# Nine chunks of keys for a tile's two heads, gates between transposes and masks, and exponentials ahead of a step's masks and signs, in a top-k attention kernel

## Chip, cores and metric

The kernel runs on one core of one Trainium2 chip. The metric is the device time of one execution in microseconds (us), as a median of several runs; lower is better. The engines are named as in the profile: PE (matmul) with its weight loads PEld, DVE (vector), ACT (activation), POOL (general), SP (issues the DMAs).

## The reference

Two blocks follow each other. Attention: for each of 8 batches and 8 heads, 576 queries and keys of 64 numbers; only the 32 largest scores of a row are kept. Then a mixture of 8 experts over the 4608 tokens of 512 numbers, where each expert keeps its 80 best tokens.

```python
scores = scale * np.matmul(q, k.transpose(0, 1, 3, 2))
kth = np.partition(scores, -top_k, axis=-1)[..., -top_k:-top_k + 1]
scores = np.where(scores >= kth, scores, -1000000000.0)
scores = scores - np.max(scores, axis=-1, keepdims=True)
attn = np.exp(scores)
attn = attn / (np.sum(attn, axis=-1, keepdims=True) + 1e-09)
x = np.matmul(attn, v)             # then (B, H, S, D) -> (B*S, H*D)
...
logits = x @ w_gate                # expert = argmax, gate = softmax there
h = np.maximum(x[tok_idx] @ w1[e], 0.0)
out[tok_idx] = gate_w[tok_idx, None] * (h @ w2[e])
```

## The kernel before, in words

The attention part works through 32 pairs of heads (n = 0 to 31: a batch and two of its heads). A pair has five tiles of queries, t = 0 to 4: four of 128 queries for both heads, and one, t = 4, that holds the last 64 queries of both heads on the two halves of the partitions. A unit is one tile of one head: nine units in a pair, 288 in all (`units` in `run`). The order is written out by hand, one `step(i)` per unit; stages of several units are interleaved, each with its lag, and no scheduler changes it. Because a pair has nine units, the stages fall on even steps in one pair and on odd steps in the next.

The stages of a tile:

- `turn` (L206): once a pair, q and k are turned by ten transposes (L204) into the score buffer `sp`, and ACT copies them out (`both`, L217). `load` and `load_v` fetch two pairs ahead on SP's queue.
- `front` (L219): eight matmuls in the trace (L229; four in the code) write the scores of both heads into `sp`, and ACT copies them into the tile `s` (L236). `sp` is made by `four` (L197): four of the eight PSUM banks, from a pool with one buffer. So fronts, turns of q and k, turns of xn and the gates' logits all take the same buffer in turn, each waiting until ACT has copied the last one out.
- `parts` and `search` (L239, L248): DVE finds the eight largest of six pieces of 96 scores (L244), from them the 24 largest of the row (L255, L263). ACT makes signs against the 24th with their sum (`sign`, L260), POOL multiplies scores and signs (`y`, L266), DVE takes the next eight (L268), and `pick` (L271) chooses the threshold.
- `below` (L275): marks the scores under the threshold, for units with odd numbers on ACT (L280) and for even ones on POOL (L282).
- `turn_w` (L302): turns the scores of the tile, keys onto partitions, by transposes (L318) into the PSUM tiles `ab` (four full chunks of 128 keys per head, one buffer) and `cc` (a fifth chunk per head, two buffers). For each head the fifth chunk takes the last 128 keys, so it overlaps the fourth by 64; the rows of V that stand for the overlap are zero. Then matmuls with the masks (L323) push the dropped scores down, and ACT takes the exponentials of `cc` (L325) and `ab` (L327) into `wT`.
- `back` (L330): forty matmuls in the trace (L338; twenty in the code) multiply `wT` with V. V has a column of ones, so the sum comes along; results lie in the same bank as `cc`.
- `over` and `divide` (L342, L352): DVE inverts the sum (`z`, L350); the product with it (`xn`) is on DVE for t = 0 and 1 (L359), on ACT for the others (L367). Only then is the buffer of `cc` free.
- `norm` (L369): when a pair is complete, writes xn to memory, turns it (L204, `sp` again; copied out at L384), multiplies by the gate's weights (L389, `sp`; copied out at L396) and hands over to `gates` on DVE.

A step first walks a string of letters: "GybGcGdGeGGzaxg" in odd steps, "GGbghHmMyGcGdGeGzax" in even ones. G is a piece of `parts`, a to h and H are parts of `search` of units at the lags in the table (e holds the sign, h and H the picks), y POOL's product, m a mask on ACT, M a mask on POOL, z `over`, x `divide`. So every step issues one sign on ACT, and every even step a mask on ACT before it. After the string come `turn_w` of the unit six steps back, `front` for four steps ahead, `back` of the unit seven steps back (ahead of `turn_w` for t = 4), a `turn` if no front was due, then a part of `norm`. `turn_w` and `front` stand in the same step; it is an odd one in even pairs (the string has a sign), an even one in odd pairs (mask and sign), with t = 4 the other way round. In the step after it `back` and a turn follow: q and k after t = 1, xn of the pair before after t = 2; the logits come after t = 4.

ACT's queue in order is therefore, for one tile: [mask] sign, xn, exponentials of cc and ab, s, and in the next step [mask] sign, and both or xT.

```python
back = dict(a=0, b=1, c=1, d=1, e=1, y=3, g=4, h=5, m=5, H=4, M=4)
for c in "GybGcGdGeGGzaxg" if i % 2 else "GGbghHmMyGcGdGeGzax":
    ...
if whole(i - LT):
    self.turn_w(*units[i - LT][:2])
```

After attention comes `finish`: routing on DVE, PE and POOL, then eight experts. The change does not touch it. A second, slow path (`lean`) is compiled as well and does not run with these inputs.

Of the kernel before, what the change touches and what calls it, by code (L numbers as in the profile page):

```python
# [21 lines left out]
FAR = 1e-30  # L22
HUGE = 2.0 ** 100
TINY = 2.0 ** -48
# [3 lines left out]
def kernel(  # L28
# [120 lines left out]
    class Attention:  # L149


        def __init__(self, stack, lean):
            self.lean = lean
            pool = lambda name, bufs, **kw: stack.enter_context(tc.tile_pool(name=name, bufs=bufs, **kw))
            self.nat, self.qkp, self.rows = pool("nat", 1), pool("qkp", 2), pool("rows", 2)
            self.small, vpool = pool("small", 7), pool("vpool", 1)
            self.ps_s, self.ps_w, self.ps_c = (pool(n, k, space=PSUM) for n, k in (("ps_s", 1), ("ps_w", 1), ("ps_c", 2)))
            self.qk, self.turned, self.lg = {}, {}, {}
            self.s, self.top, self.cnt, self.y, self.mask, self.w, self.xn = ({} for _ in range(7))
            self.thr, self.z = thr_all, z_all  # L160
            self.odd = set()


            self.vb = []
            for j in range(1 if lean else 3):
                t = vpool.tile([P, NK, 2, D + 1], F32, name=f"vb{j}")
                nc.gpsimd.memset(t[:, :, :, D : D + 1], 1.0)
                nc.gpsimd.memset(t[: P - TL, NF, :, :], 0.0)
                self.vb.append(t)

            self.xT = vpool.tile([P, NK * P], F32, name="xT")
            nc.gpsimd.memset(self.xT[:, S:], 0.0)
# [15 lines left out]
        def load_v(self, n, b, hp):  # L188
            one = bass.ds(b, 1)
            t = self.vb[n % len(self.vb)]  # L190
            for h in range(2):
                nc.sync.dma_start(
                    t[:, :NF, h, :D], v[one, 2 * hp + h, : NF * P, :].rearrange("o (c p) d -> p (o c) d", p=P))
            nc.sync.dma_start(
                t[P - TL :, NF, :, :D], v[one, 2 * hp : 2 * hp + 2, NF * P :, :].rearrange("o h p d -> p (o h) d"))

# [22 lines left out]
        def front(self, n, t):  # L219
# [10 lines left out]
            g = 2 if t < NF else 1  # L230
            s = self.rows.tile([P, 2 * S], F32, name="s", tag="s", bufs=2 if self.lean else 7)
            for h in range(g):
                self.s[i + h] = s[:, h * S : (h + 1) * S]
# [14 lines left out]
        def search(self, i):  # L248
# [24 lines left out]
            yield  # L273

        def below(self, i):  # L275

            self.top.pop(i)
            self.mask[i] = self.rows.tile([P, S], BF16, name="mask", tag="mask", bufs=4)
            if i in self.odd:
                nc.scalar.activation(self.mask[i], self.s[i], Act.Relu, bias=self.thr[:, i : i + 1], scale=-1.0)  # L280
                return
            nc.gpsimd.tensor_scalar(self.mask[i], self.s[i], self.thr[:, i : i + 1], None, op0=Alu.is_lt)  # L282

# [12 lines left out]
        def drop(self, i):  # L296

            s, top = self.s[i], self.top.pop(i)
            self.mask[i] = self.rows.tile([P, S], BF16, name="mask", tag="mask", bufs=2)
            nc.vector.tensor_scalar(self.mask[i], s, self.thr[:, i : i + 1], top[:, 0, 0:1], op0=Alu.is_lt, op1=Alu.add)  # L300

        def turn_w(self, n, t):  # L302

            i = n * UPP + 2 * t
            g = 2 if t < NF else 1
            if i == NU - 1 and not self.lean:

                ab = self.four().rearrange("p h (c r) -> p h c r", r=P)
            else:
                ab = self.ps_w.tile([P, 2, NF, P], F32, name="ab", tag="ab")  # L310
            cc = self.ps_c.tile([P, 512], F32, name="cc", tag="cc")
            keys = [slice(c * P, c * P + P) for c in range(NF)] + [slice(S - P, S)]
            dst = [[ab[:, h, c, :] for c in range(NF)] + [cc[:, h * P : (h + 1) * P]] for h in range(g)]

            for h in range(g):
                sc = self.s.pop(i + h)
                for c in range(NK):
                    nc.tensor.matmul(dst[h][c], lhsT=sc[:, keys[c]], rhs=ident, start=c == 0 or (c == NF and h == 0), stop=False,  # L318
                                     is_transpose=True, skip_group_check=True)
            for h in range(g):  # L320
                mk = self.mask.pop(i + h)
                for c in (NF, *range(NF)):
                    nc.tensor.matmul(dst[h][c], lhsT=mk[:, keys[c]], rhs=huge if i + h in self.odd else minus, start=False, stop=True, skip_group_check=True)  # L323
            wT = self.rows.tile([P, 2 * NK, P], F32, name="wT", tag="wT")
            nc.scalar.activation(wT[:, 2 * NF : 2 * NF + g, :].rearrange("p h r -> p (h r)"), cc[:, : g * P], Act.Exp,  # L325
                                 scale=scale / TINY)
            nc.scalar.activation(wT[:, : g * NF, :], ab.rearrange("p h c r -> p (h c) r")[:, : g * NF, :], Act.Exp, scale=scale / TINY)  # L327
            self.w[n, t] = wT, cc

        def back(self, n, t):  # L330

            wT, cc = self.w.pop((n, t))
            vb = self.vb[n % len(self.vb)]
            for h in range(2 if t < NF else 1):
                o = slice(2 * P + h * (D + 1), 2 * P + (h + 1) * (D + 1))
                for c in range(NK):
                    for r in range(0, P, TL):
                        nc.tensor.matmul(cc[r : r + TL, o], lhsT=wT[:, h * NF + c if c < NF else 2 * NF + h, r : r + TL],  # L338
                                         rhs=vb[:, c, h if t < NF else r // TL, :], start=(c == 0), stop=(c == NF))
            self.w[n, t] = cc  # L340

        def over(self, n, t):  # L342


            g = 2 if t < NF else 1
            sums = self.w[n, t][:, 2 * P : 2 * P + 2 * (D + 1)].rearrange("p (h d) -> p h d", h=2)[:, :g, D]
            z = self.z[:, n % NP, t, :g]
# [4 lines left out]
        def divide(self, n, t):  # L352
            if t == 0:
                self.xn[n] = self.rows.tile([P, NK, 2, D], F32, name="xn", tag="xn")
            cc = self.w.pop((n, t))
            if t < 2:

                sums = cc[:, 2 * P : 2 * P + 2 * (D + 1)].rearrange("p (h d) -> p h d", h=2)[:, :, :D]
                nc.vector.tensor_tensor(out=self.xn[n][:, t, :, :], in0=sums, op=Alu.mult,  # L359
                                        in1=self.z[:, n % NP, t, :].unsqueeze(2).to_broadcast([P, 2, D]))  # L360
                return
            for h in range(2):
                if t < NF:
                    p, o, j, m = slice(0, P), 2 * P + h * (D + 1), h, P
                else:
                    p, o, j, m = slice(TL * h, TL * h + TL), 2 * P, 0, TL
                nc.scalar.activation(self.xn[n][:m, t, h, :], cc[p, o : o + D], Act.Copy, scale=self.z[p, n % NP, t, j : j + 1])  # L367

        def norm(self, n, b, hp, bi, nb, cs=range(NK)):  # L369
# [14 lines left out]
            nc.scalar.copy(xT[:, at], ps[:, at])  # L384
            yield 1
            lp = self.four()[:, 0, : NK * E].rearrange("p (c e) -> p c e", e=E)
# [49 lines left out]
        def run(self, slow):  # L436
# [14 lines left out]
            def whole(i):  # L451

                return 0 <= i < NU and units[i][2] > 0

            def step(i, last):
# [11 lines left out]


                back = dict(a=0, b=1, c=1, d=1, e=1, y=3, g=4, h=5, m=5, H=4, M=4)
                for c in "GybGcGdGeGGzaxg" if i % 2 else "GGbghHmMyGcGdGeGzax":  # L470
                    if c == "G":
                        if 0 <= i < NU:
                            next(first[i])
                    elif c == "a":
                        if 0 <= i < NU:
                            next(first[i], None)
                            second[i] = self.search(i)
                            next(second[i])
                    elif c == "z":
                        for u in drawn:  # L480
                            self.over(*u)
                    elif c == "x":
                        for u in drawn:
                            self.divide(*u)
                    elif c in "mM":
                        if 0 <= i - back[c] < NU:
                            self.below(i - back[c])
                    elif i - back[c] in second:
                        next(second[i - back[c]])
                done = list(drawn)  # L490
# [9 lines left out]
                if rest:  # L500
                    back()
                if whole(i - LT):
                    self.turn_w(*units[i - LT][:2])

# [12 lines left out]
                for g in list(later):  # L517
                    if ready[g] and busy and not last:
                        continue
# [410 lines left out]
```

## Time and profile before

| | |
|---|---|
| three runs | 992.38, 997.87, 997.98 us; median 997.87 |
| profiled execution | 994.35 us; span from the first to the last instruction 992.5 us |
| first exponentials of the pipeline to the last front | about 37 to 830 us |
| last back of attention | 858.5 us |
| mean granted clock of PE | 0.985 |
| DVE idle, 50 to 800 us | 36 us of 750 |

The page's second part cuts the span into 40 slices of 24.8 us; each digit is a busy share in tenths:

```profile
PE   5989999898989898989898989899898988699896
...
DVE  5899999899999999999999999999999989361010
ACT  3889989998989898989998989989898988301110
POOL 3677767776777776776677677767777777201111
PEclk9999999999999999999999999999999999879998
```

Up to slice 34 attention runs, and three engines are at nine tenths together. Such rows do not say which of them sets the pace: matmuls overlap each other, and an engine that waits 100 ns between many instructions looks full. For that one reads the list of waits (engine and line that waited, what released it, us in total, times, the longest) and the timelines (start, length, engine, line, operation, output<-input, and in brackets the idle time before). Two instructions of one engine overlap in these lists; what an instruction costs its queue is the distance from its start to the start of the next.

### The profile page before, as it was taken

Reading aid. Unit: us, or ns where it says so; the run is one execution under the profiler, and the core shown is the slowest. Engines: PE = TensorE matmul, PEld = TensorE weight load, DVE = VectorE, ACT = ScalarE, POOL = GpSimd, SP = SyncE. Lnnn points to the kernel's source line nnn. Section 1 sums busy time; section 2 is a strip of 40 time slices with the busy share of each in tenths; the row PEclk is TensorE's granted clock in tenths of the full one; section 3 lists DMA queues with packets and bytes.
Section 4 is the critical chain, followed back from the end, with each engine's and each line's share of the span. In section 5 each row is a group of like instructions: output and inputs, shape, how many; then the busy total and the mean of one; then the engine's idle time right before and its main releaser. Section 6 shows DMA issues by size and latency. Waiting matters only on the chain.

```text
span 992.5 us, 35681 instructions
## 1 busy us (share of the span) xinstructions
PE 873.2 (88%) x13368; PEld 707.4 (71%) x13368; DVE 824.4 (83%) x4992; ACT 766.8 (77%) x1524; POOL 625.1 (63%) x474
## 2 busy tenths in 40 slices
PE   5989999898989898989898989899898988699896
PEld 3667777676767676777777777777676776578786
DVE  5899999899999999999999999999999989361010
ACT  3889989998989898989998989989898988301110
POOL 3677767776777776776677677767777777201111
PEclk9999999999999999999999999999999999879998
DMA  3454443333333232332222222211122200275910
GB/s 72 121 138 113 125 130 89 85 92 92 92 90 81 83 92 81 87 87 71 49 51 50 50 50 50 50 42 46 38 50 50 50 15 15 78 276 184 370 43 28
DMA packets 167798, 85.77 MB, mean 86 GB/s; under 512 B 117696, under 2 KB 154560, under 8 KB 167616
## 3 DMA queue, kind: packets, MB, share of 16 engines
q1 hardware_dynamic: 166592, 80.78, 29.0%
q0 software_dynamic: 1024, 2.62, 0.9%
q8 instruction: 107, 1.75, 0.7%
q14 instruction: 75, 0.61, 0.2%
HBM read 63.19 MB, written 20.19 MB: 84 GB/s over the span
## 4 chain that ended last, share of the span: by engine, by line
DVE 40%; PE 24%; ACT 20%; issue 9%; POOL 6%; DMA 1%; SPq 0%; POOLq 0%; DVEq 0%; ACTq 0%
DVE w L268 12%; DVE cand L244 11%; PE cc L338 7%; ACT sign L260 6%; DVE cand L263 4%; POOL y L266 4%; ACT wT L327 4%; PE yp L814 4%; ACT mask L280 4%; DVE top L255 3%; PE sp L229 3%; DVE pick L271 3%; ACT xn L367 3%; ACT wT L325 2%; PE ab L318 2%
## 5 line engine op out<-in xcount | busy, mean ns | idle before, releaser
L244 DVE MAX8 cand<-s 128x8 f32<-128x96 f32 x1728 | 400.1, 245 | 8.8 <-ACT s L236 8.8
L282 POOL TENSOR_SCALAR mask<-s,thr_all 128x576 bf16<-128x576 f32 x144 | 248.0, 1722 | 226.8 <-DVE pick L271 115.5
L266 POOL TENSOR_TENSOR y<-s,sign 128x576 f32<-128x576 f32 x288 | 363.2, 1282 | 13.8 <-ACT sign L260 13.8
L338 PEld LDWEIGHTS cc<-vb,wT 128*64 128x64 f32 x5760 | 181.6, 138 | 131.1 <-ACT wT L327 119.6
L338 PE MATMUL cc<-vb,wT 128*64 128x65 f32 x5760 | 203.9, 225 | 60.5 <-ACT wT L327 59.4
L268 DVE MAX8 w<-y 128x8 f32<-128x576 f32 x288 | 217.8, 756 | 13.8 <-POOL y L266 7.4
L260 ACT ACTIVATE sign<-s,w 128x576 bf16<-128x576 f32 x288 | 222.8, 774 | 1.2 <-DVE w L255 0.3
L229 PE MATMUL sp<-both 64*128 64x288 f32 (+1 forms) x1280 | 203.1, 437 | 6.4 <-ACT s L236 4.5
L236 ACT ACTIVATE s<-sp 128x1152 f32<-128x1152 f32 (+1 forms) x161 | 166.5, 1035 | 29.9 <-PE sp L229 29.4
L318 PE MATMUL ab<-ident,s 128*128 128x128 f32 x1148 | 177.5, 282 | 0.0
L327 ACT ACTIVATE wT<-ab 128x1024 f32<-128x1024 f32 (+1 forms) x159 | 148.8, 936 | 0.0
L229 PEld LDWEIGHTS sp<-both 64*128 64x128 f32 (+1 forms) x1280 | 106.0, 180 | 46.6 <-ACT s L236 7.9
L318 PEld LDWEIGHTS ab<-ident,s 128*128 128x128 f32 x1148 | 128.0, 142 | 10.1 <-issue 0.8
L255 DVE MAX8 top<-cand 128x8 f32<-128x48 f32 x576 | 115.4, 200 | 4.7
L280 ACT ACTIVATE mask<-s,thr_all 128x576 bf16<-128x576 f32 x144 | 111.9, 777 | 2.8 <-DVE pick L271 2.4
L263 DVE MATCH_REPLACE8 cand<-top,cand 128x48 f32<-128x48 f32 x576 | 110.6, 192 | 0.0
L323 PEld LDWEIGHTS <-mask 128*128 128x128 bf16 x1440 | 94.4, 98 | 1.9
L318 PE MATMUL cc<-ident,s 128*128 128x128 f32 x288 | 80.5, 279 | 8.4 <-ACT xn L367 8.4
L325 ACT ACTIVATE wT<-cc 128x256 f32<-128x256 f32 (+1 forms) x160 | 56.9, 356 | 26.3 <-PE cc L323 25.2
L217 ACT COPY both<-sp 128x1152 f32<-128x1152 f32 x31 | 34.8, 1124 | 29.7 <-PE sp L204 29.7
L826 POOL DMA_INDIRECT out_dram<-y,idx_s x8 | 7.4, 928 | 78.6 <-DVE y L825 78.6
L260 ACT ACTIVATION_READ_ACCUMULATOR sign<-s,w 128x1 f32 x288 | 56.6, 197 | 0.0
(188 smaller groups left out, 994.8 us busy)
## 6 DMA issues: line engine op xcount, KB each, us to landing
w<-in_moe_w_dram SPq DMA_DIRECT2D x10, 2048.0 KB, 12.0
w<-in_moe_w_dram SPq DMA_DIRECT2D x24, 512.0 KB, 3.9
out_dram<-zero SPq DMA_DIRECT2D x9, 1024.0 KB, 5.6
qn<-in_q_dram SPq DMA_DIRECT2D x64, 128.0 KB, 2.6
kn<-in_k_dram SPq DMA_DIRECT2D x64, 128.0 KB, 2.5
vb<-in_v_dram SPq DMA_DIRECT2D x64, 128.0 KB, 2.5
xd<-xn SPq DMA_DIRECT2D x32, 256.0 KB, 2.6
qn<-in_q_dram SPq DMA_DIRECT2D x32, 32.0 KB, 2.5
```

Of the source, the lines that this page charges most:

```text
L229: nc.tensor.matmul(o, lhsT=qT[d, t * P : t * P + m], rhs=kT[d, j * HS : (j + 1) * HS], start=True, stop=True)
L236: nc.scalar.activation(s[:, j * HS : (j + w) * HS].rearrange("p (j c) -> p j c", c=HS), ps[:, j : j + w, :HS], Act.Copy, scale=TINY)
L244: nc.vector.max(out=cand[:, j, :], in_=s[:, j * S // NG : (j + 1) * S // NG])
L260: nc.scalar.activation(sign, s, Act.Sign, bias=w9[:, 7:8], scale=-1.0, accum_out=cnt)
L263: nc.vector.match_replace(out=cand, in_to_replace=dst, in_values=cand, imm_value=LOW)
L266: nc.gpsimd.tensor_tensor(out=y, in0=s, in1=sign, op=Alu.mult)
L268: nc.vector.max(out=w9[:, 8:], in_=y)
L280: nc.scalar.activation(self.mask[i], self.s[i], Act.Relu, bias=self.thr[:, i : i + 1], scale=-1.0)
L282: nc.gpsimd.tensor_scalar(self.mask[i], self.s[i], self.thr[:, i : i + 1], None, op0=Alu.is_lt)
L318: nc.tensor.matmul(dst[h][c], lhsT=sc[:, keys[c]], rhs=ident, start=c == 0 or (c == NF and h == 0), stop=False, is_transpose=True, skip_gr ...
L327: nc.scalar.activation(wT[:, : g * NF, :], ab.rearrange("p h c r -> p (h c) r")[:, : g * NF, :], Act.Exp, scale=scale / TINY)
L338: nc.tensor.matmul(cc[r : r + TL, o], lhsT=wT[:, h * NF + c if c < NF else 2 * NF + h, r : r + TL], rhs=vb[:, c, h if t < NF else r // TL, ...
```

## The change

- `front` keeps the tile of both heads' scores (2 x 576 = 1152 columns) as one, and `turn_w` turns it in nine chunks of 128 for t < 4 instead of five per head. The fifth chunk holds the last 64 keys of the first head and the first 64 of the second; it alone goes into `cc`, which is now 128 wide for every tile. t = 4 stays at five.
- The masks of a tile's two heads lie in one tile (three buffers of two heads, four of one before), and all are multiplied by the same matrix `huge`, with 2^80 for 2^100.
- V is laid out to fit: keys 0 to 511 of the first head, 64 to 575 of the second, 0 to 511 of the second (for t = 4), and four chunks of which half is zero. That is six DMAs a pair for three, and two memsets per buffer for one. `back` has as many matmuls as before.
- `divide`: xn of t = 1 is made on ACT, as two copies.
- `norm` yields 2 after the copy of xT, and the logits with their copy are issued by `gate`, between the transposes and the masks of the next `turn_w` (that of t = 3).
- In `step`, `turn_w` (and `back` for t = 4 ahead of it) stands before the string. On ACT the order becomes: exponentials, [mask] sign, xn, s; on PE and DVE the order changes only by the gate, and on DVE by the later sums of `norm`.

```diff
@@ load_v
-                nc.sync.dma_start(
-                    t[:, :NF, h, :D], v[one, 2 * hp + h, : NF * P, :].rearrange("o (c p) d -> p (o c) d", p=P))
+            for j, h, k0 in ((0, 0, 0), (1, 1, TL), (2, 1, 0)):
+                nc.sync.dma_start(t[:, j * NF : (j + 1) * NF, :D],
+                                  v[one, 2 * hp + h, k0 : k0 + NF * P, :].rearrange("o (c p) d -> p (o c) d", p=P))
...
@@ below
+        def mask_of(self, i):
+            n, u = divmod(i, UPP)
+            if u % 2 == 0:
+                self.mask[n, u // 2] = self.rows.tile([P, 2 * S], BF16, name="mask", tag="mask", bufs=2 if self.lean else 3)
+            return self.mask[n, u // 2][:, u % 2 * S : (u % 2 + 1) * S]
...
@@ turn_w
-            keys = [slice(c * P, c * P + P) for c in range(NF)] + [slice(S - P, S)]
-            dst = [[ab[:, h, c, :] for c in range(NF)] + [cc[:, h * P : (h + 1) * P]] for h in range(g)]
...
+            keys = [slice(c * P, c * P + P) for c in range(2 * NF + 1)] if t < NF else [slice(c * P, c * P + P) for c in range(NF)] + [slice(S - P, S)]
+            dst = [ab[:, 0, c, :] for c in range(NF)] + [cc[:, :P]] + ([ab[:, 1, c, :] for c in range(NF)] if t < NF else [])
...
+            for c, o in enumerate(dst):
+                nc.tensor.matmul(o, lhsT=sc[:, keys[c]], rhs=ident, start=c in (0, NF, NF + 1), stop=False, is_transpose=True,
+                                 skip_group_check=True)
+            if between:
+                between()
+            for c in sorted(range(len(dst)), key=lambda c: c != NF):
+                nc.tensor.matmul(dst[c], lhsT=mk[:, keys[c]], rhs=minus if self.lean else huge, start=False, stop=True,
+                                 skip_group_check=True)
-            nc.scalar.activation(wT[:, 2 * NF : 2 * NF + g, :].rearrange("p h r -> p (h r)"), cc[:, : g * P], Act.Exp,
-                                 scale=scale / TINY)
+            nc.scalar.activation(wT[:, 2 * NF, :], cc[:, :P], Act.Exp, scale=scale / TINY)
@@ divide
-            if t < 2:
+            if t < 1:
@@ norm
             nc.scalar.copy(xT[:, at], ps[:, at])
-            yield 1
+            yield 2
@@ step, ahead of the string
+                done = list(drawn)
+                drawn.clear()
...
+                rest = whole(i - LT) and units[i - LT][2] == 2
+                if rest:
+                    back()
+                def gate():
+                    for g in later:
+                        if ready[g] == 2:
+                            ready[g] = next(g)
+                if whole(i - LT):
+                    self.turn_w(*units[i - LT][:2], gate)
...
@@ step, behind it: the same lines without the gate go; "z" and "x" use done
-                    if ready[g] and busy and not last:
+                    if (ready[g] == 1 and busy or ready[g] == 2 and i < NU + LT) and not last:
```

## The prediction

> **What bounds the kernel now.** I read the page first, then the list of waits, then PE's and ACT's timelines over two pairs of heads (429 to 486 us). The page names no single owner:
>
> ```profile
> PE 873.2 (88%) x13368; PEld 707.4 (71%) x13368; DVE 824.4 (83%) x4992; ACT 766.8 (77%) x1524; POOL 625.1 (63%) x474
> ```
>
> From 50 to 800 us the stretches of 50 us hold about 45.1 us of PE, 45.1 of ACT and 47.6 of DVE. What matters is who waits:
>
> ```profile
> PE cc L338 <- ACT wT L327: 59.4, 114, 3.3
> ...
> DVE z_all L350 <- PE cc L338: 36.1, 40, 4.2
> ...
> ACT both L217 <- PE sp L204: 29.7, 31, 2.1
> ACT s L236 <- PE sp L229: 29.4, 36, 2.4
> ...
> ACT wT L325 <- PE cc L323: 25.2, 35, 2.3
> ```
>
> PE waits for ACT, ACT waits for PE, DVE waits for PE; ACT waits for DVE hardly at all (2.4 us at L280, 0.3 at L260). So the loop PE-ACT sets the pace, though DVE looks fuller. One tile of it, PE first, then ACT:
>
> ```profile
> 454.66 1.24 PE L229 MATMUL sp<-both 64*128 64x288 f32 x8
> 456.18 1.39 PE L338 MATMUL cc<-vb,wT 128*64 128x65 f32 x40 [0.28 <-ACT wT L327]
> 457.50 0.86 PE L204 MATMUL sp<-ident,qn 128*128 128x128 f32 x5
> ...
> 460.88 1.24 PE L229 MATMUL sp<-both 64*128 64x288 f32 x8
> ```
>
> ```profile
> 457.71 0.77 ACT L260 ACTIVATE sign<-s,w 128x576 bf16<-128x576 f32 x1
> ...
> 459.18 1.12 ACT L217 COPY both<-sp 128x1152 f32<-128x1152 f32 x1 [0.61 <-PE sp L204]
> 460.21 0.77 ACT L260 ACTIVATE sign<-s,w 128x576 bf16<-128x576 f32 x1
> 460.97 0.37 ACT L325 ACTIVATE wT<-cc 128x256 f32<-128x256 f32 x1
> 461.24 1.02 ACT L327 ACTIVATE wT<-ab 128x1024 f32<-128x1024 f32 x1
> 462.16 1.13 ACT L236 ACTIVATE s<-sp 128x1152 f32<-128x1152 f32 x1
> ```
>
> Call M the start of a tile's front (L229), when the masks before it are issued. In pair 16 M falls at 450.21, 454.66, 460.88, 466.22 and 469.95 (t = 0 to 4), and pair 17 starts at 475.01: steps of 4.45, 6.22, 5.34, 3.73, 5.06, sum 24.80. The other kind of pair (15, joined to 17 at t = 1) has 5.10, 6.1, 6.00, 4.31, 5.66, sum 27.2. Two pairs are 51.98 us; the z stalls of DVE repeat at that distance (82.70, 134.67, 186.64).
>
> **Durations, start to start on the same engine.** PE: front 1.17 (444.55 to 445.72); back 1.32; turn of q and k 1.58; turn of xn 0.79; logits 0.69; transposes 1.15 for ten, so 0.11 each; masks 0.65 for ten, 0.065 each. ACT: exponentials of cc 0.27 (256 columns) and 0.17 (128, at 444.50), of ab 0.90, t = 4 0.48; s 1.03, half 0.53; mask 0.67; sign 0.76 with its accumulator read; a pair of xn 0.39; xT 0.53; both 1.02. PE to ACT 0.10; s to the next user of sp 1.18 after the start of s (471.30 to 472.48). These links give back the old path: pair 15 from its turn (430.86) to its xn turn is turn 1.58 + 0.10 + both 1.02 + mask 0.67 + sign 0.76 + cc 0.27 + ab and handover 1.07 + back 1.32 = 6.79; the trace has 437.65 - 430.86 = 6.79.
>
> **The change, part by part.**
> - Nine chunks: 128 tiles lose a transpose and a mask, 0.175 us each, 22 us of PE, counted below. ACT's cc shrinks by 0.10, 13 us in all, counted too.
> - xn of t = 1 goes from DVE (32 x 0.19 to 0.29 us) to ACT (32 x 0.39 = 12.5 us, counted). DVE's 6 to 9 us are put at nothing: it already waits 36 us for PE. Were DVE the bound, they would be gained.
> - V loads: six issues a pair for three, 0.6 us each on SP, 55 us in all. SP stands 291 us at L192 waiting for PE, and the loads run two pairs ahead: nothing; without that cover the first back of a pair would wait, up to 1.7 us x 32.
> - POOL: three more memsets (0.16 us each) ahead of an engine that then waits 12.6 us for the first sign: nothing. Masks now lie in three tiles of two heads instead of four of one; POOL's 12.3 us of waiting on PE at L282 can go, off the path.
> - Gate: the logits leave the place after t = 4, where they wait about 0.5 us for s (15.3 us in 29 times), and go between transposes and masks of t = 3, +0.69 there, with their small copy.
> - Order on ACT: exponentials, then sign (in the odd pairs mask and sign), xn, then s. Exponentials come 0.76 to 1.8 us earlier, so back no longer waits; but s now starts only after mask and sign, and sp has one buffer: the next turn (t = 1: q and k; t = 2: xn) needs that copy finished. Queued behind the exponentials, which now wait for PE's masks, are sign, mask, xn and s; PE waits for s, and for xn, which frees cc.
>
> **The new loop, steps of M (even pair / odd pair).**
> - t = 0 to 1, PE alone: 1.17 + 1.32 + nine transposes 1.04 + nine masks 0.58 = 4.11 / 4.11.
> - 1 to 2: ACT comes late: from the M before, 0.10 + 0.90 + sign, xn of t = 4, s, mask, sign (3.61) = 4.61, then 0.17 + 0.90 = 5.68, that is 1.57 after this M. Sign 0.76 (with mask 1.43), 1.18 to sp, turn 1.58, transposes and masks 1.62: 6.71 / 7.38.
> - 2 to 3: 0.10 + 0.90 + 0.76 (1.43) + xn of t = 1 0.39 + 1.18, xn turn 0.79, transposes 1.04, logits 0.69, masks 0.58: 6.43 / 7.10; in the even pair xT queues 0.14 longer: 6.57.
> - 3 to 4: 1.17 + 1.32 + 0.97 = 3.46 / 3.46.
> - 4 to 0: 0.10 + 0.48 + mask 0.67, two signs 1.52, s 1.03, xn of t = 3 0.55 = 4.35 until cc is free, then five transposes 0.55 and masks 0.58: 5.48 / 5.48.
> Sums 26.33 and 27.53, together 53.86 for 51.98: +1.88 us. Bounds: below, zero, if small idle times close; above, +2.5, since the same links leave 0.6 us of the old period unexplained and may again. I take +2.1, near the sum, which is worked from rows in every link. Of the 16 double periods 15.5 run with fronts: +33 us (29 to 39). At the end (after 836 us) no fronts stand in the way; exponentials ahead could save the 3.3 us wait at 840.15, a sign later could cost 1.2: I take nothing. The profiled execution took 994.35 us (span 992.5 and 1.85 around it): 1027 by its own time. The median of the three is 997.87, 3.5 higher: **1030**.
>
> **A clock that may fall.** PE will stand about 2.0 us at cc of each t = 0 (from M + 2.34 to M + 4.35). In the trace a wait of 0.85 us leaves the next back at 1.39 us; one of 3.28 us (840.15) is followed by a back of 2.13 and this stretch:
>
> ```profile
> 840.00:845.00 5.00, 4.85 (x63) 4.72 (x64) 2.57 (x14) 2.88 (x7) 3.69 (x3) 0.66 0.04 8
> ```
>
> So a fall costs about 1.5 us (back 0.74, transposes 0.7); 0 to 32 x 1.5 = 48 us. 2.0 is nearer to 0.85: I take 0. [...]
>
> **Rivals.**
> - Faster: s is not what PE stands on. Then the turns start at M + 2.49 for 3.34 to 4.18, and 5.0 us of two pairs go (0.85 + 1.01 and 1.51 + 1.69); PE-ACT would need 48.8 and DVE with POOL become the bound. Their own loop is pick, handover 0.17, POOL mask 1.69, two products 2.53, last maximum 0.76 and picks 0.3: 5.46 a tile (POOL's masks at 455.82, 461.28, 466.75, 472.21), nine tiles 49.1, with 0.8 of gates and sums 49.9. That is -2.1 x 15.5 = -32: 962 us, 966 by the median. For: DVE's 36 us of stalls hang on back, which comes earlier. Against: L389 already waits for s in 29 of 32 pairs. It decides once more than 1.9 of the 5.0 us fail to appear.
> - Equal: half of the +1.9 is eaten by links that ACT fills better than I think: 0 to +0.6 a double period, 994 to 1007 us.
> - Much slower: signs come after exponentials that wait, so POOL's products, which start at least 2 us after the end of their sign when both are counted off in order in the timelines, wait too and DVE falls behind; 0.4 us more a tile, 144 tiles: +58, about 1088. The clock falling in every pair (+48, 1078) ends near it. Against: DVE gains 4 us of slack a double period.
>
> **How the numbers follow.** Forecast 0.72, faster 0.14, equal 0.08, much slower 0.06. Within 1% is about what a measurement of this kernel can tell from no change, so faster 0.14, same 0.08, slower 0.78. The forecast's own range is 1015 to 1048 (bounds 0.9 to 3.0 a double period, plus 3.5 us between runs). The whole range leaves out the faster and the much slower case, 0.20: 993 to 1052.
>
> **What would show it.** Right: PE waits of about 1 us at the turns (L204's line) for s, 64 times; cc of t = 0 waiting about 2 us for xn; ACT waiting at the cc exponentials; back's 59 us gone; steps near 4.1, 6.7, 6.6, 3.5, 5.5; DVE's z stalls larger. Wrong: turns that start right after back; ACT waiting for DVE at signs; a double period under 51.

## The result and the profile after

The changed kernel takes 1049.2 us (median of four runs, 1047.56 to 1051.7) where the kernel before, run beside it, takes 997.5: a ratio of 1.0533 [1.05, 1.0566]. The forecast was 1030 with 993 to 1052. So the sign and that range held; the forecast's own, narrower range ended at 1048 and was passed by 1 us, and the loss, some 52 us, is larger than the 33 that the sum gave. The profiled execution took 1048.8 us with a span of 1047.1. Every ratio in this document is the recorded one of the fast runs with its 95% interval, which can differ by 0.3% from the quotient of the medians, and one run of "order without the gate" took 1559.07 us and is not in its ratio (without it the median there is 1020.63).

The list of waits of the kernel after has, for each engine, line and releaser, the total in us, the number of times and the longest. Its line numbers are new: L209 is a turn (before L204), L242 s, L333 the transposes, L339 the matmuls that bring the masks into PSUM, L342 and L343 the exponentials of cc and ab, L356 the back, L368 z, L385 xn on ACT, L293 the mask on ACT.

```profile
DVE z_all L368 <- PE cc L356: 68.4, 70, 2.5
...
PE sp L209 <- ACT s L242: 58.3, 61, 1.8
PE cc L333 <- ACT xn L385: 55.5, 31, 2.1
ACT wT L342 <- PE cc L339: 46.7, 56, 1.7
...
PE cc L356 <- ACT wT L343: 12.9, 17, 1.1
...
DVE gw L442 <- ACT el L433: 10.6, 3, 3.6
```

Before, PE's great wait was for the exponentials at the back (59.4 us, 114 times). That is down to 12.9 us. Two others have come in its place, and both are waits for what ACT does after the exponentials: a turn waits for s, 61 times and 58.3 us (before 1.2), and the transposes of a tile wait for xn, 31 times and 55.5 us (before 8.4). The two lines of before for these are:

```profile
PE cc L318 <- ACT xn L367: 8.4, 16, 1.1
...
PE sp L204 <- ACT s L236: 1.2, 1, 1.2
```

ACT in turn waits for PE's masks at the cc exponentials, 46.7 us for 25.2. This is PE in an even pair (14), with the idle time ahead of an instruction and its releaser in brackets:

```profile
421.82 0.66 PE L333 MATMUL ab<-ident,s 128*128 128x128 f32 x4
424.27 0.33 PE L333 MATMUL cc<-ident,s 128*128 128x128 f32 x1 [1.79 <-ACT xn L385]
...
425.46 1.24 PE L234 MATMUL sp<-both 64*128 64x288 f32 x8
...
429.98 0.22 PE L339 MATMUL cc<-huge,mask 128*128 128x128 bf16 x1 [0.81 <-ACT mask L293]
...
430.57 1.24 PE L234 MATMUL sp<-both 64*128 64x288 f32 x8
...
433.53 0.86 PE L209 MATMUL sp<-ident,qn 128*128 128x128 f32 x5 [0.39 <-ACT s L242]
...
436.74 1.24 PE L234 MATMUL sp<-both 64*128 64x288 f32 x8
...
440.11 0.86 PE L209 MATMUL sp<-ident,xn 128*128 128x128 f32 x5 [0.80 <-ACT s L242]
...
443.35 1.19 PE L234 MATMUL sp<-both 64*64 64x288 f32 x8
```

Take the fronts (L234) as M: 425.46, 430.57, 436.74, 443.35 are steps of 5.11, 6.17 and 6.61. And ACT over the first of them, from a little ahead of it, so that the first rows show what xn of t = 3 (423.70) stands behind:

```profile
421.27 1.13 ACT L242 ACTIVATE s<-sp 128x1152 f32<-128x1152 f32 x1
422.28 0.77 ACT L293 ACTIVATE mask<-s,thr_all 128x576 bf16<-128x576 f32 x1
422.94 0.77 ACT L266 ACTIVATE sign<-s,w 128x576 bf16<-128x576 f32 x1
...
423.70 0.51 ACT L385 ACTIVATE xn<-cc,z_all 128x64 f32<-128x64 f32 x2
425.18 0.28 ACT L342 ACTIVATE wT<-cc 128x128 f32<-128x128 f32 x1 [0.97 <-PE cc L339]
425.57 1.02 ACT L343 ACTIVATE wT<-ab 128x1024 f32<-128x1024 f32 x1
426.49 0.77 ACT L266 ACTIVATE sign<-s,w 128x576 bf16<-128x576 f32 x1
...
427.25 0.62 ACT L385 ACTIVATE xn<-cc,z_all 64x64 f32<-64x64 f32 x2
427.89 1.14 ACT L242 ACTIVATE s<-sp 128x1152 f32<-128x1152 f32 x1
429.06 0.77 ACT L293 ACTIVATE mask<-s,thr_all 128x576 bf16<-128x576 f32 x1
429.74 0.76 ACT L266 ACTIVATE sign<-s,w 128x576 bf16<-128x576 f32 x1
...
430.50 0.25 ACT L342 ACTIVATE wT<-cc 128x128 f32<-128x128 f32 x1
430.68 1.02 ACT L343 ACTIVATE wT<-ab 128x1024 f32<-128x1024 f32 x1
431.60 0.77 ACT L266 ACTIVATE sign<-s,w 128x576 bf16<-128x576 f32 x1
...
432.36 1.12 ACT L242 ACTIVATE s<-sp 128x1152 f32<-128x1152 f32 x1
```

From 425.57 to 433.37 ACT has no gap: between the cc of t = 0 and the turn it is ACT's queue that sets the time, and PE follows it.

The loop is regular, so the steps of M can be read off every pair. The table has the median of each step over pairs 2 to 29, even and odd pairs apart, and the sum of two pairs. "Beyond" is what all 28 pairs together lie above these medians.

| steps of M, us | 0-1 | 1-2 | 2-3 | 3-4 | 4-0 | two pairs | beyond |
|---|---|---|---|---|---|---|---|
| before, even | 4.44 | 6.22 | 5.34 | 3.73 | 5.06 | | |
| before, odd | 5.10 | 6.10 | 6.00 | 4.32 | 5.66 | 51.96 | 0.8 |
| forecast, even | 4.11 | 6.71 | 6.57 | 3.46 | 5.48 | | |
| forecast, odd | 4.11 | 7.38 | 7.10 | 3.46 | 5.48 | 53.86 | 0 |
| after, even | 5.11 | 6.17 | 6.61 | 3.47 | 5.56 | | |
| after, odd | 4.32 | 7.57 | 7.24 | 3.55 | 5.55 | 55.15 | 13.0 |

The regular loop has lost 3.19 us per two pairs, 44.7 us in these 14, and another 12.2 lie beyond it. The last front (pair 30, t = 3) starts at 889.0 us for 829.4 before, 59.6 later, while the span is 54.6 longer: the end gives about 5 us back.

### The profile page after: what moved, and what is told of

Its sections match the earlier page's. It is cut to its first block, busy times and chain, and to the rows that moved or that the text cites. A ratio compares the mean times of both kernels' runs of the same rounds, so it can differ in the third digit from the quotient of the medians.

```text
span 1047.1 us, 35499 instructions
## 1 busy us (share of the span) xinstructions
PE 879.5 (84%) x13112; PEld 696.4 (67%) x13112; DVE 814.9 (78%) x4960; ACT 783.3 (75%) x1588; POOL 627.9 (60%) x477
## 3 DMA queue, kind: packets, MB, share of 16 engines
q8 instruction: 105, 1.72, 0.7%
## 4 chain that ended last, share of the span: by engine, by line
PE 34%; ACT 25%; DVE 24%; issue 8%; POOL 7%; DMA 1%; SPq 0%; POOLq 0%; DVEq 0%; ACTq 0%
DVE w L274 9%; ACT s L242 9%; ACT sign L266 7%; DVE cand L250 5%; PE sp L234 5%; PE cc L356 5%; PE ab L333 5%; POOL y L272 4%; PE yp L839 4%; ACT xn L385 3%; PE sp L209 3%; ACT mask L293 3%; POOL mask L295 3%; PE ab L339 3%; DVE pick L277 2%
## 5 line engine op out<-in xcount | busy, mean ns | idle before, releaser
L272 POOL TENSOR_TENSOR y<-s,sign 128x576 f32<-128x576 f32 x288 | 364.9, 1281 | 44.1 <-ACT sign L266 43.7
L356 PEld LDWEIGHTS cc<-vb,wT 128*64 128x64 f32 x5760 | 186.1, 140 | 81.5 <-ACT wT L343 64.5
L356 PE MATMUL cc<-vb,wT 128*64 128x65 f32 x5760 | 208.4, 227 | 13.0 <-ACT wT L343 12.9
L234 PE MATMUL sp<-both 64*128 64x288 f32 (+1 forms) x1280 | 211.8, 452 | 6.4 <-ACT s L242 4.5
L333 PE MATMUL ab<-ident,s 128*128 128x128 f32 x1148 | 179.5, 284 | 0.0
L242 ACT ACTIVATE s<-sp 128x1152 f32<-128x1152 f32 (+1 forms) x161 | 165.2, 1027 | 12.0 <-PE sp L234 11.2
L343 ACT ACTIVATE wT<-ab 128x1024 f32<-128x1024 f32 (+1 forms) x159 | 149.2, 939 | 17.2 <-PE ab L339 14.0
L234 PEld LDWEIGHTS sp<-both 64*128 64x128 f32 (+1 forms) x1280 | 110.3, 187 | 48.7 <-ACT s L242 7.9
L333 PEld LDWEIGHTS ab<-ident,s 128*128 128x128 f32 x1148 | 128.8, 142 | 11.6 <-issue 0.8
L293 ACT ACTIVATE mask<-s,thr_all 128x576 bf16<-128x576 f32 x144 | 111.2, 772 | 0.9 <-DVE pick L277 0.5
L339 PEld LDWEIGHTS <-mask 128*128 128x128 bf16 x1312 | 86.3, 100 | 14.1 <-issue 8.6
L333 PE MATMUL cc<-ident,s 128*128 128x128 f32 x160 | 47.2, 295 | 55.5 <-ACT xn L385 55.5
L339 PE MATMUL ab<-huge,mask 128*128 128x128 bf16 x1148 | 92.3, 222 | 0.0
L368 DVE RECIPROCAL z_all<-cc 128x2 f32<-128x2 f32 (+1 forms) x160 | 25.9, 162 | 76.7 <-PE cc L356 68.4
L342 ACT ACTIVATE wT<-cc 128x128 f32<-128x128 f32 x160 | 43.8, 274 | 49.5 <-PE cc L339 46.7
L385 ACT ACTIVATE xn<-cc,z_all 128x64 f32<-128x64 f32 (+1 forms) x256 | 68.2, 307 | 1.2 <-DVE z_all L368 0.8
```

What stands on the lines that cost most here:

```text
L234: nc.tensor.matmul(o, lhsT=qT[d, t * P : t * P + m], rhs=kT[d, j * HS : (j + 1) * HS], start=True, stop=True)
L242: nc.scalar.activation(s[:, j * HS : (j + w) * HS].rearrange("p (j c) -> p j c", c=HS), ps[:, j : j + w, :HS], Act.Copy, scale=TINY)
L272: nc.gpsimd.tensor_tensor(out=y, in0=s, in1=sign, op=Alu.mult)
L293: nc.scalar.activation(mask, self.s[i], Act.Relu, bias=self.thr[:, i : i + 1], scale=-1.0)
L333: nc.tensor.matmul(o, lhsT=sc[:, keys[c]], rhs=ident, start=c in (0, NF, NF + 1), stop=False, is_transpose=True, skip_group_check=True)
L339: nc.tensor.matmul(dst[c], lhsT=mk[:, keys[c]], rhs=minus if self.lean else huge, start=False, stop=True, skip_group_check=True)
```

## The experiments

The theory on record: exponentials ahead of the string push s and xn behind mask and sign in ACT's queue; s frees sp, xn frees cc, and PE stands at both. Rivals: the gate does it (logits between transposes and masks of t = 3); the clock that falls behind the new wait; or s is not what the time hangs on. Every ratio is against the kernel before, run on the same chip.

**Order undone.** In the kernel after, `back` (t = 4) and `turn_w` go back behind the string; chunks, gate and xn of t = 1 stay.

```
-                if rest:
-                    back()
...
-                if whole(i - LT):
-                    self.turn_w(*units[i - LT][:2], gate)
                 lag = dict(a=0, b=1, c=1, d=1, e=1, y=3, g=4, h=5, m=5, H=4, M=4)
                 for c in "GybGcGdGeGGzaxg" if i % 2 else "GGbghHmMyGcGdGeGzax":
...
+                if rest:
+                    back()
+                if whole(i - LT):
+                    self.turn_w(*units[i - LT][:2], gate)
```

> The changed kernel with turn_w back behind the step's string; chunks, masks, gate and xn of t = 1 stay as changed. If the order on ACT is the cause (s and xn queued behind exponentials that wait for PE), the turns no longer wait for s: a double period near the old 52.0 us, less 8 x 0.10 for cc and plus 2 x 0.39 for xn, so 51 to 52.5 and 985 to 1000 us. If the nine chunks, the V loads, the gate's place or the extra xn on ACT cost the time, it stays near 1045.

Measured: 1008.41 us, ratio 1.0150 [1.0103, 1.0198], two pairs 52.38. Nearly three quarters of the loss go with the order, but the kernel does not come back to 997 and lies 8 us above the 985 to 1000 that were expected: a part that isn't the order costs 1.5%. The waits part the two new ones from each other. The turns no longer wait for s (1.2 us, once, as before), but the transposes still wait for xn:

```profile
PE cc L333 <- ACT xn L385: 43.0, 30, 1.7
```

So the wait for s comes with the order, and the long wait for xn with the gate: in the kernel before, the logits stood ahead of these transposes.

**Order alone.** The kernel before, with its block of `back` and `turn_w` moved ahead of the string and nothing else.

```
+                if rest:
+                    back()
+                if whole(i - LT):
+                    self.turn_w(*units[i - LT][:2])
                 for c in "GybGcGdGeGGzaxg" if i % 2 else "GGbghHmMyGcGdGeGzax":
...
-                if whole(i - LT):
-                    self.turn_w(*units[i - LT][:2])
```

> The kernel before with turn_w alone put ahead of the string; ten chunks, old masks, logits after t = 4. If the order is the cause: 1040 to 1065 us, with PE waiting for s at the turns (L204) and for xn at the cc of t = 0. If other parts of the change are: about 997.

Measured: 1028.2 us, 1.0338 [1.0303, 1.0373], two pairs 54.34 (+2.38). The old kernel with the new order alone loses some 33 us: slower by the order is shown from both sides. It is less than was expected (1040 to 1065). Of the two waits expected only one is there (lines as before):

```profile
ACT wT L325 <- PE cc L323: 94.1, 111, 2.5
...
PE sp L204 <- ACT s L236: 44.5, 61, 1.2
...
PE sp L389 <- ACT s L236: 26.6, 30, 1.5
...
PE cc L318 <- ACT xn L367: 10.3, 17, 1.8
```

PE stands for s at the turns and at the logits (L389); cc waits for xn little more than in the kernel before (10.3 us for 8.4).

**The front ahead, too.** If the price is that s stands behind mask and sign, then a front (and so its s) issued ahead of the string should pay. In the kernel after, the front moves up behind `turn_w`, so that ACT has exponentials, s, mask, sign, xn.

```
                 if whole(i - LT):
                     self.turn_w(*units[i - LT][:2], gate)
+                f = i + 4 if i not in (0, 1) else i + 3
+                busy = 0 <= f < NU and units[f][2] != 1
+                if busy:
+                    self.front(*units[f][:2])
```

> The changed kernel with front put ahead of the string as well, so that ACT does exponentials, then s, then mask, sign and xn. If PE's waits for s at the turns are what costs: the 5.0 us of a double period that the prediction named go, from 56.1 to about 51, 965 to 985 us, until DVE and POOL bound it at 49.9. If the waits for s are only a symptom and the loss hangs on the wait for xn at t = 0 and the clock behind it: no less than 1030.

Measured: 1099.49 us, 1.1071 [1.1011, 1.1131], two pairs 58.73. A clear miss for the theory in the form I gave it. The waits of this kernel say why:

```profile
POOL y L272 <- ACT sign L266: 131.0, 79, 14.9
PE cc L333 <- ACT xn L385: 96.8, 67, 2.6
...
ACT s L242 <- PE sp L234: 70.4, 124, 2.4
```

The turns no longer wait for s. But ACT now stops at s for a front that PE has only begun (124 times, 70.4 us), and mask, sign and xn stand behind this stop; xn comes later still (96.8 us for 55.5). So taking the wait for s away did not show its price: the experiment put another in its place. The wait at cc for xn grows here, but so do others (POOL's for the sign, ACT's at s), and the mean granted clock falls to 0.942; which of them costs the time, this run does not show.

**A filler for the clock.** Twelve matmuls of zeros (256 columns, bf16) into ab at t = 0, ahead of the transposes that write ab over: added work, which leaves PE standing 0.5 us in place of 1.8.

```
+            if t == 0 and n and not self.lean:
+                z = zero.bitcast(BF16)
+                for _ in range(12):
+                    nc.tensor.matmul(ab[:, 0, 0:2, :].rearrange("p c r -> p (c r)"), lhsT=z[:, :P], rhs=z, start=True, stop=True,
+                                     skip_group_check=True)
```

> The changed kernel with twelve matmuls of zeros (256 columns each, about 1.6 us in all, into ab, which the transposes then overwrite) ahead of the transposes of t = 0, so that PE stands only some 0.2 us at cc instead of 1.8. If the granted clock that falls there makes up what the sums missed (56.1 us a double period for 53.9): front and back after t = 0 at 1.17 and 1.32 us again, 1015 to 1030 us. If the clock is off the path, or does not fall for that wait: 1045 to 1052.

Measured: 1043.75 us, 1.0476 [1.0425, 1.0526]; the regular two pairs stay at 55.18. That lies between the two ranges expected, next to the one for a clock that is off the path: the clock is not where the bulk went. It is not quite nothing either. Two windows of the kernel after, each from the front of a t = 0 on, behind a wait of the same 1.79 to 1.80 us (columns: us, then busy time of PE, PEld, DVE, ACT, POOL, then the granted clock):

```profile
425.46:430.46 5.00, 4.19 (x68) 3.41 (x66) 4.08 (x24) 4.83 (x10) 3.36 (x3) 1.00 0.42 103
452.38:457.38 5.00, 5.00 (x59) 3.99 (x57) 3.40 (x24) 4.83 (x9) 3.44 (x3) 0.66 0.26 71
```

In the second the clock is 0.66 and the front and the back take 1.94 and 2.27 us for 1.24 and 1.39. Of the 30 such waits (pairs 1 to 30, 1.79 to 2.08 us) 11 are followed by a slow stretch of this kind, at 0.6 to 1.3 us each; in pairs 2 to 29 that is 7.8 us. With the filler no pair from 2 to 29 shows one behind this wait:

```profile
448.41:453.41 5.00, 5.00 (x74) 4.01 (x74) 4.92 (x35) 4.83 (x9) 3.43 (x3) 1.00 0.30 77
```

The time falls by less than these 7.8 us (5.5 by the medians, 4.6 of span). The clock, 0.981 in the mean of the execution for 0.969 in the kernel after, falls in other places there: in pairs 17 and 25, which take 4.1 us more together than in the kernel after, and in pair 27 (1.6 us).

**xn of t = 3 on DVE.** In the kernel after, the product that frees the cc for which t = 0 waits goes to DVE, where no exponentials or signs stand ahead of it.

```
-            if t < 1:
+            if t in (0, 3):
```

> The changed kernel with xn of t = 3 made on DVE, so that cc is free for t = 0 without ACT's queue. If PE's wait for xn there (3.6 us of a double period) and ACT's wait for the masks behind it are a link of the loop: the step from t = 4 to 0 falls from 5.7 to about 4.0 us and some of it comes back as lateness of ACT, 1005 to 1025 us. If the wait only moves to the exponentials, because ACT has the same work to do first: 1040 to 1050.

Measured: 990.29 us, 0.9930 [0.9904, 0.9956]. One changed condition takes back all of the loss and a little more, where 1005 to 1025 was expected: nothing of the gain comes back as lateness of ACT. Two pairs are 51.77 (-3.38), and the gain lies where the wait was: step 4-0 falls from 5.56 to 3.54 in even pairs and from 5.55 to 3.88 in odd ones. The waits that remain:

```profile
PE sp L209 <- ACT s L242: 57.4, 61, 1.8
...
PE cc L339 <- ACT mask L293: 15.5, 31, 0.8
```

No line of cc waiting for xn is left; the turns wait for s as much as before (57.4 us for 58.3), and the kernel is still no slower than the one before. This tells the two new waits apart in the kernel after: most of what the change lost hung on xn of t = 3.

**Order and gate undone.** As "order undone", with the logits back after t = 4: what remains is nine chunks, and xn of t = 1 on ACT.

```
-            yield 2
+            yield 1
...
-                    if (ready[g] == 1 and busy or ready[g] == 2 and i < NU + LT) and not last:
+                    if ready[g] and busy and not last:
```

> The kernel with turn_w behind the string again, and the logits also back behind back of t = 4: nine chunks, new masks and V, xn of t = 1 on ACT remain. If the gate's place cost the 1.2 us of a double period that the first of the two left (1008 us): the old period less cc's 0.8 plus xn's 0.4 to 0.8, about 52, 985 to 1000 us. If chunks, V loads or xn cost it: 1003 to 1010.

Measured: 991.71 us, 0.9965 [0.9942, 0.9988], two pairs 51.86. Without order and gate the loss is gone.

**Chunks alone.** The same, with xn of t = 1 on DVE again (`if t < 2`).

> As the one before with xn of t = 1 back on DVE: nine chunks, new masks and V alone. If ACT's queue is on the path of the odd and even pairs: 0.4 to 0.8 us of a double period less than with xn on ACT, 978 to 992 us, and faster than the kernel before by the 0.10 us that each cc exponential is shorter (8 x 0.10 x 15.5 = 12 us). If the shorter chunks lie beside other work: 993 to 998.

Measured: 980.12 us, 0.9836 [0.9807, 0.9866], two pairs 51.05. Nine chunks alone are a gain of 1.6%, which the rest of the change more than gives back; moving xn of t = 1 costs 0.81 per two pairs.

**Order without the gate.** The kernel after, with the logits after t = 4.

> The changed kernel with the logits back behind back of t = 4, order kept. If gate and order add up: about 1.2 us of a double period less, 1025 to 1035 us, with PE waiting for s at the logits. If the gate helps where the order makes s late: above 1049.

Measured: 1021.11 us, 1.0240 [1.0207, 1.0273], two pairs 53.58. It lies a little below the 1025 to 1035 expected. Between this kernel and the one after lies the gate alone: +1.57 per two pairs. All of that is in step 2-3, where the logits now stand: 5.79 becomes 6.61 in even pairs and 6.46 becomes 7.24 in odd ones, near the 0.69 a pair that the prediction counted. Step 4-0, which the logits have left, gives nothing back: it is 5.56 in both kernels. The waits of this kernel say why:

```profile
PE sp L407 <- ACT s L242: 26.4, 30, 1.4
...
PE cc L333 <- ACT xn L385: 10.3, 17, 1.8
```

Per two pairs the logits (L407), which stand just ahead of these transposes, wait 1.79 us for s here, and cc 0.49 for xn; with the gate cc waits 3.63. The logits had stood on part of the stretch in which xn was late. Which of the two, s or xn, holds step 4-0 without the gate is open: xn of t = 3 on DVE was not run with this order and no gate.

**Chunks, with xn of t = 3 on DVE as well.** "Chunks alone" with `if t in (0, 1, 3)`.

> Nine chunks alone (turn_w behind the string, logits after t = 4), with xn of t = 0, 1 and 3 on DVE. There cc of t = 0 waits for xn only 0.5 us of a double period, since the logits stand ahead of it; so what xn of t = 3 is worth is its time in ACT's queue, at most 0.4 a pair: 50.4 to 51.2 us, 968 to 980 us. If DVE, which is idle 1.2 us of 51.2 there, becomes the bound: 980 to 990.

Measured: 971.80 us, 0.9789 [0.9743, 0.9836], two pairs 50.64. By its median the fastest kernel of this study, ahead of both the one before and the one after.

**The same two products on DVE, order and gate kept,** and **with the gate and the old order:** the kernel after and "order undone", each with `if t in (0, 1, 3)`.

> The whole change with xn of t = 0, 1 and 3 on DVE. Against the same with t = 0 and 3 (990 us): xn of t = 1 stands between sign and s of t = 2 and cost 0.7 us of a double period in the other order, so 52.5 falls to about 51.8, 975 to 985 us. If s is not what the turn of xn waits for, no change: 988 to 992.

> turn_w behind the string, gate as changed, nine chunks, xn of t = 0, 1 and 3 on DVE. Without the order and the wait for xn at t = 0 (2.9 us of a double period in the first experiment) 53.2 falls by about 2.9 and by 0.7 for t = 1, to 49.6; DVE and POOL hold it at 50 to 50.4: 960 to 972 us. If the gate among the masks of t = 3 costs more than its cover at t = 4 gives back: above 980.

Measured: 977.95 us, 0.9831 [0.9797, 0.9864] with the order; 978.05, 0.9834 [0.9796, 0.9871] without it. The second is a miss: I thought that the gate was cheap once cc doesn't wait, and expected 960 to 972. With cc free early the order makes no difference that these runs can tell (50.96 and 50.61 for two pairs), and by their medians both lie some 6 us above the kernel that has neither order nor gate, though the intervals overlap. With the gate alone the regular loop is no longer than there (50.61 for 50.64); what is longer are the three pairs 9, 17 and 25, by 8.9 us together for 2.2 (with the order 7.8), of which more below.

## Why the prediction was right, and where its sum fell short

**The mechanism held.** What "what would show it" listed as right is there, but for the first two steps: turns that wait for s (61 of the 64 times, 58.3 us), cc of t = 0 waiting 1.79 us for xn (forecast 2.0), ACT waiting at the cc exponentials, the back's 59 us down to 12.9, DVE's z stalls up from 36.1 to 68.4. None of the three signs of "wrong" appeared. Steps 2-3, 3-4 and 4-0, taken alone, came within 0.15 us of the forecast in both kinds of pair. One part of the picture was wrong: the order was to bring both waits, and by the first two experiments the long wait for xn comes with the gate, which takes the logits from ahead of it.

**The range held in part by luck.** The loop's +3.19 lies above both upper bounds that the prediction gave (+2.5 in the sum, 3.0 in the forecast's own range, which do not agree with each other; the lower end of that range, 1015, has the 3.5 us between runs added where it should be taken off), and two terms that were put at nothing or not seen, the clock and the gates, cost some 13 us more; the end gave 5 back, and the measured time stayed 3 us under the 1052.

**The rivals.** Much slower: POOL's products do wait more for signs (43.7 us), but of that only 11.0 us come through to DVE's maxima, and the clock falls in one pair of three (behind 11 of 30 waits, to 0.50), not in each. Equal (at most 0.6 us a double period): no. Faster: its condition, that the turns don't stand on s, was not met. But its premise that the wait for s, as such, holds 5.0 us is not shown by any run: the attempt to take it away put another wait in its place and cost 50 us more, and the kernel with xn of t = 3 on DVE keeps it whole and loses nothing against the kernel before.

**"t = 0 to 1, PE alone" is the step that failed.** It said 4.11 and was 5.11 and 4.32, and in the odd pairs 1-2 was longer as well. PE is not alone there: in the ACT rows above, its mask, issued at 429.06 behind s, is what the masks of t = 1 wait for (0.81 at 429.98). In the odd pairs it is xn of t = 4, which ends at 400.29 in pair 13, just ahead of the transpose into cc at 400.34. The two steps 0-1 and 1-2 together are one chain on ACT, and that chain had two wrong durations: I took 0.39 for a pair of xn and 1.03 for s, the common ones. The pair of t = 4 takes 0.64 here (427.25 to 427.89) and s behind it 1.17 (427.89 to 429.06). Both stood in the trace of before, 0.65 at 474.99 and 1.16 at 476.83:

```profile
474.99 0.63 ACT L367 ACTIVATE xn<-cc,z_all 64x64 f32<-64x64 f32 x2
475.64 0.38 ACT L325 ACTIVATE wT<-cc 128x256 f32<-128x256 f32 x1
...
476.83 1.14 ACT L236 ACTIVATE s<-sp 128x1152 f32<-128x1152 f32 x1
477.99 0.78 ACT L260 ACTIVATE sign<-s,w 128x576 bf16<-128x576 f32 x1
```

With them the two steps are 0.39 longer; measured is 11.28 for 10.82 (even) and 11.89 for 11.49 (odd). With 0.43 from the other steps the sum misses by 1.29: 55.15 for 53.86, +3.19 for +1.88.

**The account in us.** Forecast: 2.1 x 15.5 = 33. Regular loop: 3.19 x 15.5 = 49, so 17 more. Clock: 8, where I took nothing between 0 and 48. A term that the prediction didn't have: DVE waits three times, 10.6 us in all, for the exponential of the gates (el, L433), which ACT issues behind s; the pairs after it (9, 17, 25) are 5.2 us longer together (3.4, 0.9 and 0.9). No such line stands in the waits of before. The wait alone is not the cost: "order alone" and "order without the gate" have it too (4.9 and 5.1 us), and there the three pairs are 0 and 1.8 us longer. It goes with the gate: the three pairs are 5.2 to 9.3 us longer in six of the seven kernels that have it, and 0 to 2.2 in the six without (before among them). Part of it is the clock once more: in pair 9 of the kernel after the granted clock is 0.50 from 292.36 to 299.18, in 17 and 25 it does not fall (1.00); with the filler it falls in all three, and they are 9.3 us longer. Why PE stands there is not settled; no run takes this term alone. The end: -5, where I took nothing. That makes 33 + 17 + 8 + 5 - 5 = 58 for 54.6 of span; the 3 us over come from taking the loop, measured on 14 double periods, times 15.5: outside pairs 2 to 29 the fronts fall back 2.7 us, not 1.5 x 3.19 = 4.8. The rest is the 0.8 that the kernel before itself lies beyond its medians.

**What each part is worth,** from the experiments, in us per two pairs (before 51.96):

| part | between which kernels | us |
|---|---|---|
| nine chunks | before, chunks alone | -0.91 |
| xn of t = 1 to ACT | chunks alone, order and gate undone | +0.81 |
| order | order and gate undone, order without gate | +1.72 |
| gate, under the new order | order without gate, after | +1.57 |
| sum | before, after | +3.19 |

The parts depend on one another: the order costs 2.38 in the old kernel; the gate costs 0.52 under the old order (order and gate undone to order undone, 51.86 to 52.38). Order and gate together cost 3.29 with xn of t = 1 and 3 on ACT (51.86 to 55.15) and 0.32 with both on DVE (50.64 to 50.96). With neither order nor gate the move of xn of t = 3 brings 0.41 (51.05 to 50.64), so about 3.0 of the 3.38 that it brings in the kernel after belong to order and gate. So most of the sum hangs on one link that no part of the change names: cc has two buffers, and xn of t = 3, behind the exponentials, a mask, two signs and s in ACT's queue, is what frees one for t = 0. The prediction had this link (4.35 until cc is free) and priced its step right (5.48 for 5.56), but it set the waits for s and for xn side by side, and did not ask what the one or the other would give back if it were taken away alone.

## What to carry to other kernels

When work is moved ahead in an engine's queue, list what it pushes back, and of that first the copies and products that free a PSUM buffer: here one such product on another engine (xn of t = 3 on DVE) was worth more than all that the change cost (3.38 us of a double period for 3.19). A step that is "PE alone" is so only if every operand of its last instruction is early too; follow the other engine's queue through it, with the duration of each shape from its own row, since one operation had 0.39 and 0.65, another 1.03 and 1.16 in the same trace. And an experiment that removes a wait by moving its cause shows the sum of both moves, not the price of the wait.

## What the runs showed of the hardware

The clock fell behind waits of PE of only 1.8 us, which I had put with the harmless 0.85: in 11 of 30 nearly equal cases, each time to a granted 0.50 for 3.41 us (the 0.66 above is the mean over 5 us), at 0.6 to 1.3 us a fall. In the trace of the kernel after the starts of the 11 slow stretches (87.56, 114.86, 169.48 and so on to 872.62) lie whole multiples of 3.413 us apart (8, 24 and so on to 230 behind the first). Divide the whole time into pieces of 3.413 us that start at such points: 15 of the 30 waits lie within one piece, to 0.05 us, and 11 of these 15 are followed by a fall. The other 15 lie across the end of a piece, and none of them is. This is the piece around one wait and the next piece:

```profile
449.37:452.78 3.41, 1.61 (x19) 1.44 (x20) 3.27 (x21) 2.33 (x7) 3.41 (x3) 1.00 0.56 127
452.78:456.19 3.41, 3.41 (x44) 2.52 (x42) 2.25 (x14) 3.37 (x7) 2.10 (x3) 0.50 0.33 94
```

In the pieces ahead of the 11 falls PE is busy 1.39 to 1.62 us of 3.41. That share alone does not decide: four pieces with 1.61 or 1.62 are not followed by a fall (the one from 422.06 is one).
